# One table of places for the side work of a fused FNet and GEGLU kernel, up to the second block of gate and up

## The chip, the cores and the metric

The kernel runs on one core of one Trainium2 chip. The metric is the device time of one execution in microseconds (us); where several executions were timed, their median is given.

## What is computed

The reference takes 2048 tokens of 448 features through two residual layers:

```
x  = A_x
n  = layernorm(x)
a  = n @ dft_hid_re.T          b = n @ dft_hid_im.T
h  = x + dft_seq_re @ a - dft_seq_im @ b
m  = layernorm(h)
h2 = h + (gelu_tanh(m @ w_gate) * (m @ w_up)) @ w_down      # 448 -> 1792 -> 448
```

## The kernel before

**Arithmetic.** Every operand is kept as two f16 parts, high and low, and a product takes three matmuls (high by high, high by low, low by high). Most products are made in the seven-product way of Strassen, so that operands are first added and subtracted among each other. The high part is a copy on ScalarE (ACT), L108 (`hi_part`), the low part a subtraction on VectorE (DVE), L112 or L114 (`lo_part`), the sums run on VectorE (L263 to L272 for tokens, L357 to L380 for the weights of gate and up, L510 to L512 for the sequence matrix, L616 to L619 for the tokens of the fast units) or on GpSimd (POOL; L232 to L235 for down's weights). SyncE (SP) issues all DMAs in one queue.

**First stage: 64 units** (`N_STEPS`), counted by `n`. A unit is a chunk of the sequence DFT: its matrix chunk `wr` is loaded (`seq_load`, L471), split into `ws` and multiplied with the normalized tokens `xs`. Units 0 to 31 are 24 plain matmuls of 448 columns (`seq_mm`, L682). Units 32 to 63 (`FAST` on) are 42 matmuls of 224 columns (`fast_mm`, L560); for each of them VectorE makes `sums` (L510 to L512) and the low parts of `ws` (L114), ScalarE the high parts. Results go out as `zs`, are turned by four DMA transposes (`z_turn`, L707) and multiplied with the hidden DFT in groups of 21 matmuls (`hid_mm`, L768, into a bank `y` that `hid_seed`, L749, fills first and `hid_out`, L757 to L759, empties), which gives the rows `h` of eight token tiles, q and j.

**Second stage: gate and up.** `GateUp(t)` for t = 0 to 41: block 0 (t = 0 to 13) has 1024 tokens in matmuls of 512 columns, the blocks 1 and 2 (t = 14 to 27, 28 to 41) have 512 each in matmuls of 256. One t is `x1, z1, y1, x2, z2, y2, y3` (L1112), where `y3` of t comes behind `x1` and `z1` of t + 1. ScalarE and VectorE empty the banks between: `pY` from `pX` (L1157), `m5` (L1163), `u2` (L1168), `g1` (L1173), `c12` and `hs` (`plus`, L1122; L1191), GpSimd multiplies (L1206). The hidden activations `hs` are written to DRAM (L1212). In blocks 1 and 2 the down projection (`dn_mm`, L1316) is woven in.

**Side work.** What prepares later operands has to be put between these products: in block 0 the split of gate and up's weights (`Weights`: raw load, `tails`, `sums`, `hi`, `rest`, `lo`, `store`) for the even chunks 2 to 12, the split of down's weights `wd` (`down_load`, `down_sums`, `down_hi`, `down_lo`), and the operands of the second block's tokens (`ffn_bias`, `ffn_norm_act`, `ffn_sums`, `ffn_hi`, `ffn_lo`, and four DMA transposes `ffn_transpose`, L327, into `hops`). The token tile of q = 2, j = 0 is named `xn_2_0`, `tt_2_0`, `xs_2_0`.

**What sets the order.** No scheduler moves anything: an engine runs its instructions in the order in which the program text records them. In the first stage tables (`W_AT` for weights, `P_AT` for turns and hidden products, `F_AT` for tokens' operands, `T_AT` for the fast units' second tiles) say at which place a step is recorded: places 3n, 3n + 1 and 3n + 2 lie before unit n, after its first half and after its end. In the second stage three ways stand beside each other: the weights' steps and down's steps are written out in the loop over t (`w`, `n`, `PREP_AT`), and the tokens' steps go by `AT_A` and `AT_B` with `do(t, k)`.

Of the kernel before, what the change touches and what calls it, by code (L numbers as in the profile page):

```python
# [32 lines left out]
def kernel(  # L33
# [1307 lines left out]
    side = {}  # L1341

    def do(t, k):
        for what in side.pop((t, k), ()):
            what()
# [4 lines left out]
    AT_B = ((0, 1), (0, 3), (1, 1), (1, 3), (2, 1), (2, 2), (2, 3), (2, 3))  # L1350
    AT_B += ((3, 2), (3, 3), (4, 1), (4, 3), (4, 4), (5, 1), (5, 4), (6, 4))
    for q, t0, step, when in ((2, 5, 3, AT_A), (3, 14, 6, AT_B)):
        for j in range(2):
            plan = (
                lambda q=q, j=j: ffn_bias(q, j),
                lambda q=q, j=j: ffn_norm_act(q, j, hp[q, j]),
                lambda q=q, j=j: ffn_sums(q, j, (0,)),
                lambda q=q, j=j: ffn_hi(q, j, (0,)),
                lambda q=q, j=j: ffn_sums(q, j, (1,)),
                lambda q=q, j=j: ffn_lo(q, j, (0,)),  # L1360
                lambda q=q, j=j: ffn_hi(q, j, (1,)),
                lambda q=q, j=j: ffn_sums(q, j, (2,)),
                lambda q=q, j=j: ffn_transpose(q, j, (0,)),
                lambda q=q, j=j: (ffn_lo(q, j, (1,)), ffn_sums(q, j, (3,))),
                lambda q=q, j=j: ffn_lo(q, j, (2,)),
                lambda q=q, j=j: ffn_transpose(q, j, (1,)),
                lambda q=q, j=j: ffn_hi(q, j, (2,)),
                lambda q=q, j=j: ffn_transpose(q, j, (3,)),
                lambda q=q, j=j: ffn_lo(q, j, (3,)),
                lambda q=q, j=j: ffn_transpose(q, j, (2,)),  # L1370
            )
            for (f, k), what in zip(when, plan):
                at(side, (t0 + step * j + f, k), what)

# [281 lines left out]
```

## Time and profile before

| what | value |
|---|---|
| median of 3 executions | 702.33 us (701.72 to 702.81) |
| the profiled execution | 703.34 us |
| its span on the core | 701.6 us |
| granted TensorE clock | 0.999 |
| PE busy | 689.0 us, 98% |
| DVE busy | 579.9 us, 83% |
| ACT busy | 417.2 us, 59% |
| POOL busy | 109.8 us, 16% |
| DMA moved | 155.43 MB |

Busy time is the time in which an engine has an instruction under way. A matmul of the profile lasts until its modelled end, so two neighbours overlap. In the views below, a wait is the idle time of an engine just before an instruction, with the engine and line that ended it; a timeline row has the start, the duration, the engine, the line, operation, what is written and read, how many instructions were merged, and in brackets the idle time before.

### The profile page before, as it was taken

To read this page: it belongs to the slowest core of one execution; us is meant where nothing else is said; L and a number is where in the kernel's file an instruction comes from. 1 tells how busy PE (TensorE), PEld (TensorE's weight loads), DVE (VectorE), ACT (ScalarE), POOL (GpSimd) and SP (SyncE) were. 2 spreads that over 40 slices of the span, in tenths; PEclk is the share of its full clock that TensorE was granted. 3 is DMA by queue.
4 is the path that set the end of the run, shared out by engine and by line. 5 is a ranking of instruction groups with operands and counts; after the bars stand their busy time and mean duration, and the time that the engine had idled before them with its cause. 6 is when DMAs were issued, how large, how long until landed. Compare 5 with 4: busy or idle time off the path is not lost. (4 is left out here: it accounts for less than half of the span.)

```text
span 701.6 us, 13978 instructions
## 1 busy us (share of the span) xinstructions
PE 689.0 (98%) x5266; PEld 508.7 (73%) x5266; DVE 579.9 (83%) x1203; ACT 417.2 (59%) x855; POOL 109.8 (16%) x127
## 2 busy tenths in 40 slices
PE   9999999999999999999999999999999999999998
PEld 5555555554979879887744444459999999999997
DVE  7998799948999798997548999976788876899786
ACT  5776677837766475664637778556555454555631
POOL 0000001010100100000213333421020111232224
PEclk9999999999999999999999999999999999999999
DMA  8788559797887729675564679797899985887612
GB/s 283 248 227 282 155 207 269 247 258 264 182 204 164 187 92 175 203 180 185 150 227 138 244 258 322 193 308 247 238 255 257 320 275 178 309 303 265 243 40 81
DMA packets 115781, 155.43 MB, mean 222 GB/s; under 512 B 63744, under 2 KB 80256, under 8 KB 115712
## 3 DMA queue, kind: packets, MB, share of 16 engines
q1 hardware_dynamic: 115712, 154.53, 72.9%
q8 instruction: 41, 0.67, 0.4%
q14 instruction: 28, 0.23, 0.1%
HBM read 105.74 MB, written 34.34 MB: 200 GB/s over the span
## 5 line engine op out<-in xcount | busy, mean ns | idle before, releaser
L1112 PEld LDWEIGHTS <-gw 128*128 128x128 f16 x1330 | 129.9, 98 | 44.5 <-issue 3.4
L682 PE MATMUL acc<-xs,ws 128*128 128x448 f16 x768 | 146.5, 352 | 0.4 <-DVE xs L149 0.4
L560 PEld LDWEIGHTS <-ws 128*128 128x128 f16 x1344 | 128.1, 98 | 7.5 <-DVE ws L114 5.8
L682 PEld LDWEIGHTS <-ws 128*128 128x128 f16 x768 | 75.1, 98 | 70.5 <-issue 0.3
L1316 PE MATMUL acc_d<-wd,dn_w 128*128 128x224 f16 x1008 | 110.8, 259 | 0.3 <-DVE dn_w L112 0.3
L1316 PEld LDWEIGHTS <-dn_w 128*128 128x128 f16 x1008 | 96.8, 98 | 2.7 <-DVE dn_w L112 0.5
L1206 POOL TENSOR_TENSOR hs<-hs,c 128x256 f32<-128x256 f32 (+1 forms) x42 | 60.1, 1431 | 244.7 <-ACT c L1204 212.5
L560 PE MATMUL acc_f<-t,ws 128*128 128x224 f16 x768 | 93.0, 259 | 1.7 <-DVE ws L114 1.7
L1112 PE MATMUL pY<-hops,gw 128*128 128x256 f16 (+1 forms) x560 | 85.6, 294 | 2.3 <-ACT u L1168 1.5
L114 DVE SCALAR_TENSOR_TENSOR ws<-wr,ws 128x768 f16<-128x768 f32 (+2 forms) x66 | 69.8, 1059 | 8.4 <-ACT ws L108 8.4
L560 PE MATMUL acc_f<-xs,ws 128*128 128x224 f16 x576 | 74.0, 259 | 1.7 <-DVE ws L114 1.7
L108 ACT ACTIVATE ws<-wr 128x768 f16<-128x768 f32 (+2 forms) x66 | 60.4, 916 | 15.0 <-DMA wr<-in_w_seq_dram 14.1
L768 PE MATMUL y<-wh,z 128*128 128x448 f16 x336 | 66.2, 352 | 1.1 <-ACT y L749 1.1
L1112 PE MATMUL pX<-hops,gw 128*128 128x256 f16 (+1 forms) x385 | 61.7, 294 | 0.0
L1112 PE MATMUL pZ<-hops,gw 128*128 128x256 f16 (+1 forms) x385 | 61.7, 294 | 0.0
L768 PEld LDWEIGHTS <-z 128*128 128x128 f16 x336 | 32.9, 98 | 30.6 <-issue 1.3
L108 ACT ACTIVATE ws<-sums 128x512 f16<-128x512 f32 x64 | 39.0, 624 | 24.4 <-DVE sums L510 19.3
L1157 ACT ACTIVATE pY<-pX 128x256 f32<-128x256 f32 (+1 forms) x42 | 18.4, 439 | 56.4 <-PE pX L1112 56.4
L1122 DVE SCALAR_TENSOR_TENSOR c<-pZ,u 128x256 f32<-128x256 f32 (+1 forms) x42 | 21.4, 510 | 36.0 <-PE pZ L1112 18.3
L1112 PEld LDWEIGHTS <-gu_w 128*128 128x128 f16 x266 | 26.0, 98 | 31.8 <-issue 0.9
L213 POOL TENSOR_SCALAR r_h<-mv_h 128x2 f32<-128x2 f32 x7 | 1.7, 240 | 267.0 <-ACT y L759 266.9
L1168 ACT ACTIVATE u<-pY 128x256 f32<-128x256 f32 (+1 forms) x42 | 19.1, 454 | 40.7 <-PE pY L1112 40.3
(160 smaller groups left out, 1023.3 us busy)
## 6 DMA issues: line engine op xcount, KB each, us to landing
gw<-w_dram SPq DMA_DIRECT2D x35, 896.0 KB, 6.7
wr<-in_w_seq_dram SPq DMA_DIRECT2D x100, 256.0 KB, 4.1
hid_dram<-hs SPq DMA_DIRECT2D x27, 512.0 KB, 6.3
hid<-hid_dram SPq DMA_DIRECT2D x54, 256.0 KB, 5.4
w_dram<-gu_w SPq DMA_DIRECT2D x14, 896.0 KB, 4.7
wr<-in_w_seq_dram SPq DMA_DIRECT2D x14, 512.0 KB, 5.5
gu_raw<-in_w_gu_dram SPq DMA_DIRECT2D x14, 384.0 KB, 5.5
gu_raw<-in_w_gu_dram SPq DMA_DIRECT2D x14, 320.0 KB, 5.1
```

Of the source, the lines that this page charges most:

```text
L108: A.activation(dst, src, AF.Copy, scale=scale)
L114: V.scalar_tensor_tensor(dst, src, scale, hi, op0=ALU.mult, op1=ALU.subtract)
L213: G.tensor_scalar(r[:, 1], mv[:, :, 1], D * EPS, -0.5 / (D * X_SC**2), op0=ALU.add, op1=ALU.mult)
L560: PE.matmul(fast_sum(n, k), fast_a(n, i, lw, a), fast_b(j, lx, b), start=j == 0 and m == 0 and k in (0, 1, 3, 5), stop=j == NT // 2 - 1 an ...
L682: PE.matmul(acc[key][:, :D], w[:, lw, block * P : (block + 1) * P], xs[c][:, lx, :], start=c == 0 and m == 0, stop=c == NT - 1 and m == 2,)
L768: PE.matmul(y[:, :D], z[p][:, lz, k, g * P : (g + 1) * P], wh[:, lw, k, :], start=p == NP - 1 and k == 0 and m == 0, stop=k == 6 and m == ...
L1112: PE.matmul(ps, w[:, wo, :], ops[:, OPS[b] + m, :], start=first and n == 0, stop=last and n == len(W_TERMS[a]) - 1, skip_group_check=True,)
L1122: V.scalar_tensor_tensor(dst, ps, SC, other, op0=ALU.mult, op1=ALU.add)
L1157: A.activation(self.Y, self.X, AF.Copy)
L1168: A.activation(self.u2, self.Y, AF.Copy, scale=SC)
L1206: G.tensor_mul(c22, c22, self.cols(self.c12))
L1316: PE.matmul(ps, w[:, la, a, :], wd[n][:, lb, b, :], start=n == 0 and m == 0 and opens, stop=n == NC - 1 and m == 2, skip_group_check=True,)
```

## The change

All side work up to the second block of gate and up now stands in the tables, and one list `slots` carries it through both stages. The second stage has eight places for each t: place 192 + 8t + k, with k = 0 before `y1`, 1 behind `y1`, 2 behind `x2`, 3 behind `z2`, 4 behind `y2`, 5 behind `x1` of t + 1, 6 and 7 at the end of t. The steps of the even weight chunks are rows of `W_AT` now, down's weights have a table `D_AT`, the second and third block's tokens a table `H_AT`, and `do(q)` is called at each place. Nothing is computed that was not computed before, and no step is left out: the instructions are the same on every engine. What differs is where some of them stand: `rest` of a weight chunk now comes ahead of the low parts of the raw weights; in the first stage second tiles (`T_AT`), turns and hidden products (`P_AT`), tokens' operands (`F_AT`) and chunks 0 and 1 (`W_AT`) have other numbers; in the second stage the tokens of q = 2 and down's first and last chunks stand elsewhere.

```diff
     W_AT = {
...
-        1: (0, 70, 79, 81, 84, 84, 87, 87, 91),
-        0: (0, 79, 88, 90, 96, 96, 99, 99, 106),
+        1: (0, 70, 79, 81, 84, 84, 84, 87, 87, 88),
+        0: (0, 78, 87, 89, 95, 95, 95, 99, 99, 106),
+        2: (2, 175, 192, 192, 193, 193, 194, 194, 197, 198),
...
     P_AT = {
...
-        4: (121, 120, 126, 133, 145, 150, 148),
-        5: (145, 144, 150, 157, 169, 186, 172),
+        4: (120, 119, 125, 132, 144, 149, 153),
+        5: (147, 147, 152, 159, 170, 187, 173),
...
     F_AT = {
...
-        2: (108, 111, 114, 114, 114, 114, 114, 114, 114, 114, 118, 119, 121, 122),
+        2: (108, 111, 111, 111, 111, 111, 111, 111, 111, 111, 116, 119, 121, 124),
...
     T_AT = {
...
-        2: (63, 86, 88),
+        2: (68, 92, 94),
...
+    H_AT = {
+        4: (225, 226, 228, 230, 230, 231, 233, 233, 248, 245, 251, 256, 252, 256, 252, 260),
+        5: (259, 260, 268, 273, 273, 274, 276, 276, 281, 284, 284, 289, 285, 289, 285, 293),
...
+    D_AT = {
+        0: (192, 195, 203, 204, 203, 206, 206),
...
+    FFN = 3 * N_STEPS
+    JIT_F = [f for f, when in W_AT.items() if f == 0 or when[4] >= FFN]
...
             lambda f=f: gu[f].hi(True),
-            lambda f=f: (gu[f].lo(True), gu[f].rest()),
+            lambda f=f: gu[f].rest(),
+            lambda f=f: gu[f].lo(True),
             lambda f=f: gu[f].hi(False),
...
+    for n, when in D_AT.items():
+        plan = (
+            lambda n=n: down_load(n),
+            lambda n=n: down_sums(n),
+            lambda n=n: down_hi(n, 0),
+            lambda n=n: down_lo(n, 0),
+            lambda n=n: down_hi(n, 1),
+            lambda n=n: down_lo(n, 1, slice(0, 2)),
+            lambda n=n: down_lo(n, 1, slice(2, 5)),
+        )
...
+    for p, when in H_AT.items():
+        o = divmod(p, 2)
+        plan = (
+            lambda o=o: ffn_bias(*o),
+            lambda o=o: ffn_norm_act(*o, hp[o]),
+            lambda o=o: ffn_sums(*o, (0,)),
+            lambda o=o: ffn_hi(*o, (0,)),
...
+    def do(q):
+        for what in slots.pop(q, ()):
+            what()
...
-    AT_A = ((0, 1), (0, 2), (0, 3), (1, 1), (1, 1), (1, 2), (1, 3), (1, 3))
-    AT_A += ((2, 1), (2, 3), (2, 3), (3, 1), (2, 4), (3, 1), (2, 4), (3, 4))
...
-        if w:
-            w.tails()
-            w.sums()
+        do(FFN + 8 * t)
         cur.y1()
...
+        do(FFN + 8 * t + 1)
         cur.x2()
-        if n is not None:
-            down_hi(n, 1)
...
+        do(FFN + 8 * t + 2)
         cur.z2()
-        do(t, 1)
+        do(FFN + 8 * t + 3)
         cur.y2()
-        do(t, 2)
+        do(FFN + 8 * t + 4)
         cur.c_last()
```

Three places show how instructions moved. The first is ScalarE in the first stage, ahead of the sums of unit 33, where the bank of the hidden product `y_2_1` gets its seed (`t2_3` are second tiles of the fast units, `gu_w1` the split weights of chunk 1). Before:

```order
L108 ACTIVATE gu_w1_1803<-gu_raw1_1526 128x256
L108 ACTIVATE t2_3_1834<-tx2_1353 128x448 x2
L108 ACTIVATE gu_w1_1803<-gu_s1_1744 128x768
L108 ACTIVATE gu_w1_1803<-gu_s1_1744 128x640
L757 ACTIVATE hx1_0_1646,mv_h1_0_1876<-y_2_0_1738 128x448
L758 ACTIVATE mv_h1_0_1876<-mv_h1_0_1876 128x1
L759 ACTIVATE y_2_0_1738,mv_h1_0_1876<-y_2_0_1738,mv_h1_0_1876 128x448
L749 ACTIVATE y_2_1_1880<-hx1_0_1646 128x448
L108 ACTIVATE gu_raw0_1717<-gu_raw0_1717 64x128 x2
L108 ACTIVATE ws33_0_1899<-wr33_1732 128x768
```

Now:

```order
L108 ACTIVATE gu_w1_1803<-gu_raw1_1519 128x256
L108 ACTIVATE gu_w1_1803<-gu_s1_1741 128x768
L108 ACTIVATE gu_w1_1803<-gu_s1_1741 128x640
L108 ACTIVATE gu_raw0_1701<-gu_raw0_1701 64x128 x2
L757 ACTIVATE hx1_0_1663,mv_h1_0_1875<-y_2_0_1761 128x448
L758 ACTIVATE mv_h1_0_1875<-mv_h1_0_1875 128x1
L759 ACTIVATE y_2_0_1761,mv_h1_0_1875<-y_2_0_1761,mv_h1_0_1875 128x448
L749 ACTIVATE y_2_1_1879<-hx1_0_1663 128x448
L108 ACTIVATE ws33_0_1900<-wr33_1730 128x768
L108 ACTIVATE ws33_1_1901<-sums33_1899 128x512 x2
L108 ACTIVATE t2_3_1937<-tx2_1471 128x448 x2
```

The two copies into `t2_3` moved from ahead of the seed to behind it, and two short copies of chunk 0's raw weights moved ahead of it.

The second is SyncE's queue in the fast units, where the matrix chunk of unit 45 (`wr45`) is loaded (`hops0<-xs_1_0` turns a token tile's operands, `z4<-zs4` the result of units 32 to 39). Before:

```order
L742 DMA hx2_0_2630<-in_x_dram 128x2x448
L707 DMA_TRANSPOSE z4_2653<-zs4_2235 128x7x128 x4
L327 DMA_TRANSPOSE hops0_1616<-xs_1_0_2454 128x4x128
L327 DMA_TRANSPOSE hops0_1616<-xs_1_0_2454 128x12x128
L471 DMA wr45_2692<-in_w_seq_dram 128x512 x2
```

Now:

```order
L471 DMA wr44_2620<-in_w_seq_dram 128x512 x2
L707 DMA_TRANSPOSE z4_2632<-zs4_2235 128x7x128 x4
L327 DMA_TRANSPOSE hops0_1665<-xs_1_0_2398 128x4x128
L471 DMA wr45_2691<-in_w_seq_dram 128x512 x2
L327 DMA_TRANSPOSE hops0_1665<-xs_1_0_2398 128x12x128
```

The load moved ahead of the widest of the four transposes.

The third is VectorE in block 0, t = 4 and 5 (`gu_w6` are split weights, `wd2` down's weights, `hs` the hidden activations, `tt_2_0` and `xs_2_0` the second block's first token tile). Before:

```order
L1122 SCALAR_TENSOR_TENSOR hs_4_4735<-pY_4_4663,m5_4_4678 128x4x128
L114 SCALAR_TENSOR_TENSOR gu_w6_4710<-gu_s6_4698,gu_w6_4710 128x384
L114 SCALAR_TENSOR_TENSOR gu_w6_4710<-gu_s6_4698,gu_w6_4710 64x3x128
L114 SCALAR_TENSOR_TENSOR gu_w6_4710<-gu_s6_4698,gu_w6_4710 64x128
L114 SCALAR_TENSOR_TENSOR gu_w6_4710<-gu_s6_4698,gu_w6_4710 128x256
L1191 SCALAR_TENSOR_TENSOR hs_4_4735<-pY_4_4663,g1_4_4720 128x4x128
L114 SCALAR_TENSOR_TENSOR wd2_4268<-wd32_2_4523,wd2_4268 128x448
L1122 SCALAR_TENSOR_TENSOR c12_5_4806<-pZ_5_4760,u2_5_4787 128x512
L243 SCALAR_TENSOR_TENSOR mv_h2_0_2924<-mv_h2_0_2924,r_h2_0_3316 128x2
L1122 SCALAR_TENSOR_TENSOR hs_5_4809<-pY_5_4745,m5_5_4766 128x4x128
```

Now, from the first of the four `gu_w6` on:

```order
L114 SCALAR_TENSOR_TENSOR gu_w6_4710<-gu_s6_4698,gu_w6_4710 128x384
L114 SCALAR_TENSOR_TENSOR gu_w6_4710<-gu_s6_4698,gu_w6_4710 64x3x128
L114 SCALAR_TENSOR_TENSOR gu_w6_4710<-gu_s6_4698,gu_w6_4710 64x128
L114 SCALAR_TENSOR_TENSOR gu_w6_4710<-gu_s6_4698,gu_w6_4710 128x256
L265 TENSOR_TENSOR tt_2_0_4746<-xn_h2_0_4728 128x192
L266 TENSOR_TENSOR tt_2_0_4746<-xn_h2_0_4728,tt_2_0_4746 128x192
L112 TENSOR_TENSOR xs_2_0_4778<-xn_h2_0_4728,xs_2_0_4778 128x2x64
L112 TENSOR_TENSOR xs_2_0_4778<-xn_h2_0_4728,xs_2_0_4778 128x2x192
L1248 SCALAR_TENSOR_TENSOR hs_4_4739<-pY_4_4663,g1_4_4721 128x4x128
L114 SCALAR_TENSOR_TENSOR wd2_4262<-wd32_2_4523,wd2_4262 128x448
L268 TENSOR_TENSOR tt_2_0_4746<-xn_h2_0_4728,tt_2_0_4746 128x192
L1179 SCALAR_TENSOR_TENSOR c12_5_4824<-pZ_5_4766,u2_5_4801 128x512
```

Five instructions of the second block's tokens came in here, and one more (L263) stands just ahead of the first `gu_w6`; `hs_5` follows `c12_5` at once, and the short one of L243 has gone further up.

More of the change, by code (lines that the diff above doesn't have):

```diff
@@ L882 @@
             put(q, what)
-    for f, n in zip(JIT_F, (6, 5)):
-        put(3 * (N_STEPS - n) + 1, lambda f=f: gu.update({f: Weights(f, f % 3)}))
-    put(3 * (N_STEPS - 3) + 2, lambda: gw_first(1))
+    if 1 not in JIT_F:
+        put(GW1, lambda: gw_first(1))
+    for n, when in D_AT.items():
[8 more added lines that the diff above has]
+        )
+        for q, what in zip(when, plan):
+            put(q, what)
+    for p, when in H_AT.items():
[5 more added lines that the diff above has]
+            lambda o=o: ffn_hi(*o, (0,)),
+            lambda o=o: ffn_sums(*o, (1,)),
+            lambda o=o: ffn_lo(*o, (0,)),
+            lambda o=o: ffn_hi(*o, (1,)),
+            lambda o=o: ffn_sums(*o, (2,)),
+            lambda o=o: ffn_transpose(*o, (0,)),
+            lambda o=o: (ffn_lo(*o, (1,)), ffn_sums(*o, (3,))),
+            lambda o=o: ffn_lo(*o, (2,)),
+            lambda o=o: ffn_transpose(*o, (1,)),
+            lambda o=o: ffn_hi(*o, (2,)),
+            lambda o=o: ffn_transpose(*o, (3,)),
+            lambda o=o: ffn_lo(*o, (3,)),
+            lambda o=o: ffn_transpose(*o, (2,)),
+        )
+        for q, what in zip(when, plan):
+            put(q, what)
+    def do(q):
+        for what in slots.pop(q, ()):
+            what()
     put(3 * (N_STEPS - 1), gelu_table)
-    put(3 * (N_STEPS - 2) + 1, lambda: (down_load(0), down_load(1)))
     fast_at = [FAST + n for n in (-4, -2, -1)] + list(range(FAST + 1, N_STEPS - 2))
@@ L967 @@
             x_lo(n + 2)
-        for what in slots.pop(3 * n, ()):
-            what()
+        do(3 * n)
         if n >= FAST:
@@ L991 @@
                 if m in (6, 13):
-                    for what in slots.pop(3 * n + 1 + m // 7, ()):
-                        what()
+                    do(3 * n + 1 + m // 7)
             continue
@@ L1021 @@
                     z_out(*key)
-            for what in slots.pop(3 * n + 1 + half, ()):
-                what()
-    assert not slots, sorted(slots)
+            do(3 * n + 1 + half)
+    assert min(slots) >= FFN, min(slots)
     last_lo.pop()()
     z_turn(NP - 1)
-    down_sums(0)
     h_tile(NB - 1, 1)
@@ L1338, in dn_store @@
         nc.sync.dma_start(outr[p // 4, p % 4], hr[p])
[L1341 to L1345, printed above, removed]
-    AT_A = ((0, 1), (0, 2), (0, 3), (1, 1), (1, 1), (1, 2), (1, 3), (1, 3))
-    AT_A += ((2, 1), (2, 3), (2, 3), (3, 1), (2, 4), (3, 1), (2, 4), (3, 4))
[L1350 to L1373, printed above, removed]
     right.close()
@@ L1398 @@
                 hid_load(d)
-        if t > 0 and w is None:
+        if t + 2 not in JIT_F:
             gw_load(t + 2)
@@ L1435 @@
         cur.x1()
-        if w:
-            w.lo(False)
-            gw[t + 2] = w.w
-        if n is not None:
-            for part in W_LO1:
-                down_lo(n, 1, part)
-        if t + 1 in PREP_AT and t > 0:
-            down_sums(PREP_AT[t + 1])
+        do(FFN + 8 * t + 5)
         if t == NF - 1:
@@ L1467 @@
             dn_sums(2)
-        do(t, 3)
-        if w:
-            w.store()
-        if w and w.f + 4 in JIT_F:
-            gu[w.f + 4] = Weights(w.f + 4, (w.f + 4) % 3)
-        if n is not None and 2 <= n + 2 < NC:
-            down_load(n + 2)
-        do(t, 4)
+        do(FFN + 8 * t + 6)
+        do(FFN + 8 * t + 7)
     COUNT = (1, 2, 1, 2, 1, 1, 2, 1, 2, 1, 2, 1, 2, 2)
@@ L1503 @@
             prev.store()
+        do(FFN + 8 * t)
         cur.y1()
@@ L1506 @@
             cur.z1()
+        do(FFN + 8 * t + 1)
         cur.x2()
@@ L1512 @@
             dn_hi(split)
+        do(FFN + 8 * t + 2)
         cur.z2()
-        do(t, 1)
+        do(FFN + 8 * t + 3)
         cur.y2()
@@ L1543 @@
             dn_sums(d)
-        do(t, 2)
-        do(t, 3)
-        do(t, 4)
+        for k in range(4, 8):
+            do(FFN + 8 * t + k)
         for p, t0 in ended.items():
```

33 lines of the change are left out of this document (11 added, 22 removed), and 37 rows, old and new, of tables (D_AT, F_AT, H_AT, P_AT).

## The prediction

> **What bounds the kernel now.** I read the page's busy times first:
>
> ```profile
> PE 689.0 (98%) x5266; PEld 508.7 (73%) x5266; DVE 579.9 (83%) x1203; ACT 417.2 (59%) x855; POOL 109.8 (16%) x127
> ```
>
> TensorE has work under way for 98% of the span and its instructions don't change, so only its waits can be won. They are few. These are PE's waits in the stretches 160 to 230, 230 to 300 and 395 to 460 us, in this order (total, times, longest):
>
> ```profile
> PE acc_f L560 <- DVE ws L114: 1.2, 2, 0.8
> PE y L768 <- ACT y L749: 1.1, 1, 1.1
> ...
> PE acc_f L560 <- DVE ws L114: 2.2, 6, 0.5
> ...
> PE pY L1112 <- ACT u L1168: 1.0, 1, 1.0
> PE pY L1112 <- ACT pY L1157: 0.4, 1, 0.4
> PE pY L1112 <- DVE hs L1122: 0.4, 1, 0.4
> ```
>
> A wait costs more than its idle time, because a matmul's modelled end overlaps the next one. In the chain of waits 102 matmuls of 224 columns take 9.75 us, one each 96 ns, while the group gives each 259 ns:
>
> ```profile
> 669.77 9.75 PE acc_d L1316 x102
> ...
> L1316 PE MATMUL acc_d<-wd,dn_w 128*128 128x224 f16 x1008 | 110.8, 259 | 0.3 <-DVE dn_w L112 0.3
> ```
>
> So 259 - 96 = 0.163 us of every wait is hidden in the busy time. With it the three stretches hold 2.3 + 3 x 0.163 = 2.8 us, 2.2 + 6 x 0.163 = 3.2 us and 1.8 + 3 x 0.163 = 2.3 us: 8.3 us in all. That is the most that this change can win.
>
> **Stretch A, 160 to 230 us (term -1.5).** ScalarE and VectorE here, from two timelines, and VectorE's load in 180 to 200 us (third number pair):
>
> ```profile
> 165.50 1.04 ACT L108 ACTIVATE t<-tx 128x448 f16<-128x448 f32 x2 [2.08 <-DMA w_dram<-gu_w]
> 166.44 1.45 ACT L108 ACTIVATE gu_w<-gu_s 128x768 f16<-128x768 f32 x2
> 169.44 0.55 ACT L749 ACTIVATE y<-hx 128x448 f32<-128x448 f32 x1
> 170.02 0.64 ACT L108 ACTIVATE gu_raw<-gu_raw 64x128 f32<-64x128 f32 x2
> ...
> 167.93 1.79 DVE L114 SCALAR_TENSOR_TENSOR gu_w<-gu_s,gu_w 128x384 f16<-128x384 f32 x4 [2.03 <-ACT gu_w L108]
> ...
> 180.00:200.00 20.00, 18.79 (x174) 16.37 (x173) 19.38 (x38) 12.60 (x28) 2.46 (x6) 1.00 1.07 210
> ```
>
> ScalarE stands 2.08 us for the store that frees `t2_3`'s buffer, then copies for 166.44 - 165.50 = 0.94 us; behind it wait chunk 1's copies and the seed at 169.44, for which TensorE waits 1.1. With the copies behind the seed 3.0 us go, and chunk 0's two copies of 0.64 come in ahead of it: the seed comes 2.4 earlier, so its wait of 1.1 + 0.16 goes. VectorE had sat 2.03 us for the same copies and was then 97% busy (19.38 of 20) up to the wait for `ws` at 192; it starts that run 2.03 earlier. TensorE arrives 1.3 earlier, so of the 1.2 + 0.33 there 1.5 + 1.3 - 2.03 = 0.8 stays. That makes 2.8 - 0.8 = 2.0. The loads of `wr31` and `wr32`, on which this stretch starts, and two transposes of `hops0` also changed places in SyncE's queue, which may shift it either way. I take -1.5, bounds -0.5 to -2.8, the whole of what the stretch holds.
>
> **Stretch B, 230 to 300 us (term -1.9).** SyncE's queue and VectorE's waits:
>
> ```profile
> 229.84 2.83 SPq L327 DMA_TRANSPOSE hops<-xs  x2
> ...
> 238.14 0.69 DVE L510 TENSOR_TENSOR sums<-wr 128x512 f32<-128x512 f32 x1 [4.69 <-DMA wr<-in_w_seq_dram]
> ...
> 266.42 7.28 SPq L707 DMA_TRANSPOSE z<-zs  x4
> 275.10 1.00 SPq L471 DMA_DIRECT2D wr<-in_w_seq_dram  x2
> ...
> 279.12 0.69 DVE L510 TENSOR_TENSOR sums<-wr 128x512 f32<-128x512 f32 x1 [2.06 <-DMA wr<-in_w_seq_dram]
> 285.82 0.69 DVE L510 TENSOR_TENSOR sums<-wr 128x512 f32<-128x512 f32 x1 [1.07 <-DMA wr<-in_w_seq_dram]
> ```
>
> VectorE sits 4.69 us for `wr45` and only then falls behind TensorE. The load now stands ahead of the wider of two transposes that took 2.83 us of SyncE; by their widths (12 and 4) it goes up by 2.83 x 12/16 = 2.1 us, so VectorE's sitting shrinks to about 2.6 and its chain starts 2.1 earlier. The moves in `F_AT` and `P_AT` put VectorE's work for tokens ahead of other sums; they fill no other idle time and I cost them at nothing. Later `wr53` goes ahead of four `z` transposes of 7.28 us, so the wait of 2.06 goes; `wr54` stays behind them, and its 1.07 grows as VectorE comes earlier. Of the 3.2 us 1.1 stays if all the 2.1 is kept; part of what is won at 242 to 257 comes back at 264 to 290, where TensorE now arrives earlier than the late `wr54`. I take -1.9, bounds -0.5 to -3.2.
>
> **Stretch C, block 0 (term -1.0).** First VectorE before the waits near 426 and ScalarE before the one of 1.0 at 449; then VectorE at t = 4 and 5, the same four `gu_w` instructions at t = 8, TensorE behind `hs`, and durations for what moves (minimum, median and maximum; then means of forms):
>
> ```profile
> 419.38 0.75 DVE L112 TENSOR_TENSOR xs<-tt,xs 128x576 f16<-128x576 f32 x1
> 421.08 0.68 DVE L1191 SCALAR_TENSOR_TENSOR hs<-pY,g 128x512 f32<-128x512 f32 x1
> ...
> 448.48 0.42 ACT L108 ACTIVATE xs<-tt 128x256 f16<-128x256 f32 x1 [4.28 <-DVE tt L272]
> 448.95 0.58 ACT L1168 ACTIVATE u<-pY 128x512 f32<-128x512 f32 x1
> ...
> 393.00 4.52 DVE L114 SCALAR_TENSOR_TENSOR gu_w<-gu_s,gu_w 128x384 f16<-128x384 f32 x4
> 399.38 0.69 DVE L1122 SCALAR_TENSOR_TENSOR hs<-pY,m 128x512 f32<-128x512 f32 x1
> ...
> 426.32 1.80 DVE L114 SCALAR_TENSOR_TENSOR gu_w<-gu_s,gu_w 128x384 f16<-128x384 f32 x4
> ...
> 401.33 1.46 PE L1112 MATMUL pY<-hops,gw 128*128 128x512 f16 x6
> ...
> L263 DVE TENSOR_TENSOR tt<-xn_h x8: 347/351/1425, 124.8 to 522.8; 128x192 f32<-128x192 f32 x8
> L265 DVE TENSOR_TENSOR tt<-xn_h x8: 348/350/353, 125.1 to 529.7; 128x192 f32<-128x192 f32 x8
> ...
> L112 DVE TENSOR_TENSOR xs<-xn_h,xs 128x128 f16<-128x128 f32 x16 | 4.5, 282 | 0.0
> L112 DVE TENSOR_TENSOR xs<-xn_h,xs 128x384 f16<-128x384 f32 x8 | 4.4, 552 | 0.1
> ```
>
> Gone: from 419.38 to 421.08 VectorE works 1.7 us on `xs_2_0`, and the waits of 0.4 + 0.4 + 0.33 = 1.1 us follow; that work now lies an iteration earlier. ScalarE stands 4.28 us for `xs_2_1`'s last copy and `u`, for which TensorE waits 1.0 + 0.16, stands behind it; the copy has moved behind the next t's `pY`. That makes -2.3. What is late next: `hs_5`. It ended at 399.38 + 0.69 = 400.07, and TensorE needs its bank from 401.33, a slack of 1.26. Six instructions came in ahead: L263, L265 and, of the same form, L266 and L268 of 0.35 each, and two of 0.28 and 0.55 (the first at most the 128x128 form's), together 2.23, less the short one that left. Without GpSimd in the way `hs_5` is 2.2 - 1.26 = 0.9 late at most. But the four `gu_w` take 4.52 us here and 1.80 at t = 8: the difference is GpSimd's four operations that run in between, and L263 shows one instruction of 0.35 stretched to 1.4. One such stretch makes it 2.0. I take +1.3, bounds 0.4 to 2.0, and -2.3 + 1.3 = -1.0.
>
> The Trainium skill ("SBUF — State Buffer", section on the two separate sides) says that an instruction of VectorE with two SBUF inputs and one of GpSimd lock each other out for the whole instruction. The trace agrees (1.80 against 4.52 us). By that rule every added instruction could take its turn behind one of GpSimd; that is the third rival.
>
> **The second block's start (term +0.8).** SyncE before it; its four transposes between 440 and 470 us with their first and last start, and their time to landing (minimum, median, maximum); the first product that reads them; VectorE's last instruction on `hs_11`; SyncE's waits for such; and the median landing of such stores there:
>
> ```profile
> 450.61 6.47 SPq L327 DMA_TRANSPOSE hops<-xs  x3
> ...
> L327 SPq DMA_TRANSPOSE hops<-xs x4: 1260/2439/3417, 438.8 to 455.8; - x4
> ...
> DMA to landing us min/median/max: 2.5/5.5/5.9
> ...
> 467.05 0.71 PE L1112 MATMUL pX<-hops,gw 128*128 128x256 f16 x5
> ...
> 454.30 0.69 DVE L1191 SCALAR_TENSOR_TENSOR hs<-pY,g 128x512 f32<-128x512 f32 x1
> ...
> SPq L1212 <- DVE hs L1191: 7.5, 3, 5.4
> ...
> hid_dram<-hs SPq DMA_DIRECT2D x3, 512.0 KB, 8.4
> ```
>
> The last three transposes of `xs_2_1` are issued from 450.61 to 457.08, the last from 455.8 (5.2 behind the first), and their product starts at 467.05. In the new table they stand behind three `hid` loads, a weight load and the store of `hs_11`, which came behind them until now, and that store waits for VectorE, here until 454.30 + 0.69 = 454.99. With stretch C's 1.0 that is 454.0, and the product is at 466.0. So the transposes are issued from 454.0 or a little later, the last 5.2 on, at 459.2 or later, and with 2.5 to 5.9 us it lands at 461.7 to 465.1: no wait. With the store's 8.4 it lands at 467.6, 1.6 late, and a late start of SyncE comes on top. So 0 to 2.2; I take 0.8, between nothing and the landing at 8.4, because the queue is fuller now where they stand.
>
> **The sum.** -1.5 - 1.9 - 1.0 + 0.8 = -3.6. The profiled execution took 703.34 us (its span 701.6 and 1.7 around it), 1.0 above the median of the three runs. The sum is a difference, so I take it off the median: 702.33 - 3.6 = 698.7 us (699.7 against the profiled one). All terms at their good ends give -2.8 - 3.2 - 1.9 + 0 = -7.9, which would need every wait of three stretches to vanish; at their bad ends -0.5 - 0.5 - 0.3 + 2.2 = +0.9.
>
> **Rivals.**
>
> *The waits only move (701.4 us, chance 0.10).* VectorE has 18 to 19 of 20 us of work in these stretches, so what it delivers earlier at 242 it may owe at 264 and 290, where `wr54` still comes late, and in block 0 `hs_5` takes what `hs_8` gave back. Then B and C are worth about nothing, the second block's start costs 0.6 and A gives 1.5: -0.9. For it speaks the busy share; against it that VectorE has 2.03 + 2.1 + 2.06 us of idle time that is really filled.
>
> *The second block starts late (704.9 us, 0.08).* One mechanism, in SyncE's queue near 455: the store of `hs_11` now stands ahead of the transposes, and SyncE's wait for such a product lasted up to 5.4 us. If the store waits so much longer than to 454.0, the transposes land at 465.1 + 5.4 = 470.5, or with the store's 8.4 at 467.6 + 5.4 = 473.0, 7.0 behind the product's 466.0: -4.4 + 7.0 = +2.6. It decides from a stall of 4.4 us on. Against it: `hs_11` is done 12 us ahead of the product in this trace, and nothing in the change delays it.
>
> The Trainium skill ("DMA: Bandwidth & Descriptors", section on queues, rings and completion order) says that each DMA engine takes descriptors in the order of its ring. [...]
>
> *VectorE and GpSimd alternate at t = 4 and 5 (701.9 us, 0.04).* If each of the four instructions behind the last `gu_w` and L263 ahead of it meets a GpSimd operation, three more are stretched by 1.07: 1.3 + 3.2 = 4.5 at `hs_5`, and the sum is -0.4. Against it: GpSimd has four operations there, and the four `gu_w` use them up already.
>
> **How the numbers follow.** The forecast has 0.78: -1.4 to -5.5, likeliest -3.6. A measurement can tell about 0.2%, 1.4 us, from no change. Faster by more than that is the forecast: 0.78. Within it lie the first and the third rival: 0.14. Slower: 0.08. The range goes from 697.0 (5.3 less) to 701.5, where it takes in the first rival and leaves out the third and the second, and about 0.07 of the forecast's own good end.
>
> **What would show it.** Right: no wait for `y` L749 near 168; the wait for `ws` near 192 below 0.8; `sums` waiting for `wr45` less than 3 us and at most one short wait between 240 and 260; none near 426 and 449; a new wait of about a microsecond on `hs` L1122's line between 396 and 402. Wrong: waits for `ws` between 260 and 292 of 2 us or more, a wait on `hops` at the first products of 256 columns above 2 us, or `wr45` landing as late as before.

## The result, and the profile after

Over 11 executions of each kernel the median went from 702.33 to 698.48 us, a ratio of 0.9948 (95% interval 0.9933 to 0.9964). The forecast was 698.7, in a range of 697.0 to 701.5. The number came out, but two of its four terms were too small a gain and one too small a cost, by a cause that it did not name; that the sum met the median is in part luck, as the account below shows.

The profiled execution of the changed kernel took 697.04 us, its span is 695.2. These are the first row of its page's busy times and all its waits of TensorE (total, times, longest, in us):

```profile
PE 687.0 (99%) x5266; PEld 509.4 (73%) x5266; DVE 575.9 (83%) x1203; ACT 416.9 (60%) x855; POOL 113.8 (16%) x127
```
```profile
PE acc_d L1373 <- DVE dn_w L112: 1.7, 1, 1.7
PE pY L1169 <- DVE hs L1179: 1.5, 2, 1.0
PE pw L102 <- POOL sign_t L93: 1.4, 1, 1.4
PE pY L1169 <- ACT u L1225: 0.4, 1, 0.4
PE acc_d L1373 <- ACT v L1107: 0.2, 1, 0.2
```

From 160 to 300 us nothing is left: no `ws`, no `y`. With the prediction's 0.163 us of hidden overlap for each wait, stretch A went from 2.8 to 0, stretch B from 3.2 to 0. In block 0 the three waits of 2.3 in all gave way to one of 1.0 + 0.16 = 1.2 on `hs`, so -1.1. The wait for `dn_w` at the second block's start went from 0.3 to 1.7, so +1.4. That is -5.7; the end has 0.3 less (0.5 to 0.2 for `v`) and the start no wait for `xs` (0.4), which makes about -6.4, as the spans have it: 695.2 - 701.6.

VectorE shows where stretches A and B were won. Its load from 160 to 180 and from 220 to 240 us (busy time is the third number), first in the kernel before, then in the changed one:

```profile
160.00:180.00 20.00, 17.64 (x33) 1.00 0.62 229
220.00:240.00 20.00, 15.04 (x24) 1.00 0.97 228
```
```profile
160.00:180.00 20.00, 19.55 (x37) 1.00 1.08 270
220.00:240.00 20.00, 18.97 (x29) 1.00 0.76 178
```

VectorE is not faster; it stands still less, 1.9 us less in the first and 3.9 less in the second. The load of `wr45` in SyncE's queue, before and now, and VectorE's sitting for it now:

```profile
232.77 3.95 SPq L471 DMA_DIRECT2D wr<-in_w_seq_dram  x6
```
```profile
226.70 1.00 SPq L471 DMA_DIRECT2D wr<-in_w_seq_dram  x2
```
```profile
230.77 0.69 DVE L510 TENSOR_TENSOR sums<-wr 128x512 f32<-128x512 f32 x1 [0.72 <-DMA wr<-in_w_seq_dram]
```

The sitting is 0.72 us where it was 4.69.

Why is the span 6.4 us shorter and the median only 3.9? The profiled execution before lies 1.0 above its median, that of the changed kernel is the fastest of its eleven. Five of the eleven have a granted clock of 0.998 and took 699.3 to 700.4 us, six have 1.0 and took 697.0 to 698.5. What the five are likely to have in common came out of the first experiment.

### The profile page after: what moved, and what is told of

The parts are those of the page before. It is cut to its first block, busy times and chain, and to the rows that moved or that the text cites. A ratio compares the mean times of both kernels' runs of the same rounds, so it can differ in the third digit from the quotient of the medians.

```text
span 695.2 us, 13978 instructions
## 1 busy us (share of the span) xinstructions
PE 687.0 (99%) x5266; PEld 509.4 (73%) x5266; DVE 575.9 (83%) x1203; ACT 416.9 (60%) x855; POOL 113.8 (16%) x127
## 4 chain that ended last, share of the span: by engine, by line
PE 91%; DVE 3%; DMA 3%; ACT 1%; issue 1%; SPq 0%; DVEq 0%; ACTq 0%
PE acc L682 21%; PE acc_f L560 19%; PE acc_d L1373 15%; PE pY L1169 12%; PE y L768 9%; PE pZ L1169 8%; PE pX L1169 8%; DVE gu_w L114 1%; DMA hid_dram<-hs 1%; DMA gw<-w_dram 1%; ACT gu_w L108 0%; DMA x<-in_x_dram 0%; SPq L327 0%; ACT u L1225 0%; DVE hs L1179 0%
## 5 line engine op out<-in xcount | busy, mean ns | idle before, releaser
L112 DVE TENSOR_TENSOR dn_w<-dn_s,dn_w 128x640 f16<-128x640 f32 x48 | 42.0, 874 | 1.6 <-ACT dn_w L108 1.6
```

Source lines behind the costliest of these rows:

```text
L112: V.tensor_sub(dst, src, hi)
```

## The experiments

Each was timed against the kernel before on the same chip; ratios are to that kernel. Numbers of places and rows are those of the changed kernel's tables.

| run | ratio | 95% interval |
|---|---|---|
| the changed kernel again | 0.9951 | 0.9936 to 0.9966 |
| changed, `t2_3` ahead of the seed | 1.0037 | 1.0022 to 1.0052 |
| changed, `F_AT` row 2 back | 0.9988 | 0.9975 to 1.0002 |
| changed, `H_AT` rows 4 and 5 back | 0.9914 | 0.9901 to 0.9928 |
| changed, `H_AT` row 5 back | 0.9918 | 0.9904 to 0.9931 |
| changed, one store on ScalarE's queue | 0.9915 | 0.9902 to 0.9929 |
| changed, rows 4 and 5 back, two copies later | 0.9921 | 0.9908 to 0.9935 |
| before, two rows of tables | 0.9945 | 0.9933 to 0.9958 |
| before, two rows and the weights' rows | 0.9924 | 0.9910 to 0.9939 |
| before, `F_AT` row 2 alone | 0.9962 | 0.9949 to 0.9975 |
| changed, store moved, six places later | 0.9904 | 0.9888 to 0.9920 |
| the last, and transposes early again | 0.9886 | 0.9869 to 0.9902 |

**The changed kernel again.**

> The changed kernel once more, unaltered, to see what of its trace is the kernel's and what is one execution's. In the two traces the waits of TensorE shrank by 6.3 us (13.2 to 6.9, start to start), but the medians by 3.85 only. Theory 1 (the waits that went are the kernel's; the profiled pair lies 1.0 above and 1.4 below its medians): the ratio to the kernel before is again 0.993 to 0.996, the waits near 168, 192, 243 to 257, 426 and 448 stay away in this trace too, those near 395 (1.18) and 467 (1.87) are there within 0.5. Rival (the stretch from 160 to 300 us was free of waits by luck of one execution, and the waits of 2 to 3 us that the forecast left there come in most executions): this trace has waits for ws of 1 us or more in sum between 190 and 292.

No wait for `ws` came back, so the rival is out: stretches A and B are free in this execution too. The wait at `dn_w` is longer than expected (2.4 + 0.16, against 1.87 "within 0.5"), and something follows it. TensorE's waits from 465 to 475 us, and that stretch in TensorE's load (busy time, count, granted clock, DMA share, GB/s):

```profile
PE acc_d L1373 <- DVE dn_w L112: 2.4, 1, 2.4
```
```profile
465.00:475.00 10.00, 7.57 (x57) 0.83 0.96 338
```

The granted clock of these 10 us is 0.83, which costs some 1.7 us beside the 2.4 + 0.16 of the wait. In the changed kernel's first trace the wait was 1.7 and the same stretch has 1.00:

```profile
465.00:475.00 10.00, 8.29 (x81) 1.00 1.03 399
```

1.7 of 698.7 us is 0.24%, which fits the clock of 0.998 that five of the six executions here have over their whole span. So executions are likely to part into two groups by what happens at that one wait; only one of the 0.998 was traced. The wait's price is 1.9 us without, and about 4.3 with the slower clock. (The kernel before has there 0.3 + 0.16.)

**`t2_3` ahead of the seed again.**

```diff
-        2: (68, 92, 94),      # T_AT
+        2: (68, 86, 88),
```

> The changed kernel with the two copies of chunk 2 to t2_3 back ahead of the seed of y_2_1 (places 86 and 88 in place of 92 and 94), nothing else undone. Theory 1 (stretch A's 2.8 us came from this move alone): the wait for y L749 near 168 and the waits for ws near 192 come back, 2.0 to 2.8 us slower than the changed kernel (or up to 6 if the copies now wait longer for the store of the chunk than they did in the kernel before). Rival (VectorE, loaded to 97% up to 192, hands on what it saves, so that the seed's delay is met by a later wait that was there anyhow): under 0.8 us slower, no wait at 168 above 0.5.

Measured 1.0037, 0.86% over the changed kernel's 0.9951, which is 6.0 us. ScalarE's copies, TensorE's bank group behind the seed, and its clock:

```profile
168.28 1.04 ACT L108 ACTIVATE t<-tx 128x448 f16<-128x448 f32 x2 [5.58 <-DMA w_dram<-gu_w]
```
```profile
173.75 6.50 PE L768 MATMUL y<-wh,z 128*128 128x448 f16 x21 [4.67 <-ACT y L749]
```
```profile
170.00:180.00 10.00, 6.25 (x21) 0.66 0.52 174
```

The copies stand 5.58 us for the store, not 2.08. SyncE shows why: the store stands behind two transposes of `hops0` that the changed kernel has moved ahead of it.

```profile
156.29 7.14 SPq L327 DMA_TRANSPOSE hops<-xs  x2
163.54 0.52 SPq L400 DMA_DIRECT2D w_dram<-gu_w  x1
```

So in the changed kernel's queue this place costs 4.7 + 0.16 for the seed, and 2.4 more for the clock behind it: the same 21 matmuls take 4.14 us in the changed kernel and 6.50 here. That is 7.3 us where 6.0 were measured; in this trace the wait at `dn_w` is 2.1 with the full clock behind it, which gives back part of what it costs in most executions of the changed kernel.

```profile
168.53 4.14 PE L768 MATMUL y<-wh,z 128*128 128x448 f16 x21
```

No wait for `ws` came behind it, against the expectation. The copies' place ahead of the seed is the cause of the wait at 168; the wait at 192 needs another.

**`F_AT` row 2 as before.**

```diff
-        2: (108, 111, 111, 111, 111, 111, 111, 111, 111, 111, 116, 119, 121, 124),
+        2: (108, 111, 114, 114, 114, 114, 114, 114, 114, 114, 118, 119, 121, 122),
```

> The changed kernel with only F_AT's row 2 as before, so that the load of wr45 stands again behind the transposes of hops0 of 4 and 12 blocks. Theory 1 (stretch B's 3.3 us came from the place of this load): VectorE waits 4 us or more for wr45 again, the waits for ws between 240 and 258 come back with 2.0 to 2.7 us in sum, and the time is 1.9 to 2.7 us longer than that of the changed kernel. Rival (VectorE's earlier work, moved in F_AT's other rows and P_AT, made the room): under 0.8 us longer, VectorE waits 4 us for wr45 and TensorE doesn't wait.

VectorE sits 3.96 us for `wr45` again, and five waits for `ws` are back (total, times, longest, from 236 to 292 us):

```profile
PE acc_f L560 <- DVE ws L114: 1.7, 5, 0.4
```

1.7 + 5 x 0.163 = 2.5 us, and the time is 0.9988 - 0.9951 = 0.37%, 2.6 us, longer. The theory holds in size, not in place: one of the five waits (0.4) stands between 240 and 258, where 2.0 to 2.7 were expected, and four (1.3) between 261 and 288. The row holds more than the load's neighbour: eight steps of ScalarE's and VectorE's on `xs_1_0` and two transposes change places with it.

**Both tiles of the second block's tokens back.**

```diff
-        4: (225, 226, 228, 230, 230, 231, 233, 233, 248, 245, 251, 256, 252, 256, 252, 260),
-        5: (259, 260, 268, 273, 273, 274, 276, 276, 281, 284, 284, 289, 285, 289, 285, 293),
+        4: (235, 236, 238, 243, 243, 244, 246, 246, 251, 254, 254, 259, 255, 259, 255, 263),
+        5: (259, 260, 262, 267, 267, 268, 270, 270, 275, 278, 278, 283, 279, 283, 279, 287),
```

> The changed kernel with the tokens' operands of the second block at their places of before (H_AT rows 4 and 5), so that of the change in blocks 0 and 1 nearly nothing is left. Theory 1 (there what is won is given back: 0.52 + 0.55 near 426 and 1.20 near 448 against 1.18 near 395 and 1.43 more near 467, together -0.3): those first three waits come back, the other two go or shrink to 0.5, and the time is within 0.7 us of the changed kernel. Rival, as in the forecast's terms (-1.0 and +0.8): 0.2 us slower than the changed kernel, with a wait at 467 as large as in it, since TensorE's earlier arrival makes it and not the order of the transposes.

Both missed. It is 0.37% faster than the changed kernel, 2.6 us, where "within 0.7" was expected. The waits that were to come back did, and from 380 on none is left at `dn_w`:

```profile
PE pY L1169 <- ACT u L1225: 1.1, 1, 1.1
PE pY L1169 <- DVE hs L1179: 0.8, 1, 0.8
PE pY L1169 <- ACT pY L1214: 0.4, 1, 0.4
```

These cost 2.3 + 0.49 = 2.8 us, against 1.2 for `hs` and 1.9 to 4.3 for `dn_w` in the changed kernel. What was missed is the price of the wait at `dn_w`, clock and all, in most executions. So this part of the change loses against the old places.

**Which part of it, and how.** In the changed kernel VectorE waits for a store, its `dn_w` stands behind that instruction, and TensorE waits for `dn_w`:

```profile
468.20 0.42 DVE L1179 SCALAR_TENSOR_TENSOR hs<-pY,m 128x256 f32<-128x256 f32 x1 [2.39 <-DMA hid_dram<-hs]
468.54 0.41 DVE L112 TENSOR_TENSOR dn_w<-hid,dn_w 128x256 f16<-128x256 f32 x1
469.01 0.56 PE L1373 MATMUL acc_d<-wd,dn_w 128*128 128x224 f16 x4 [1.71 <-DVE dn_w L112]
```

The kernel before had 0.76 us of such a wait there:

```profile
467.69 0.69 DVE L1122 SCALAR_TENSOR_TENSOR hs<-pY,m 128x512 f32<-128x512 f32 x1 [0.76 <-DMA hid_dram<-hs]
```

SyncE's queue ahead of it, and VectorE's last instruction on `hs_12`, the tile that the store writes out:

```profile
446.67 1.98 SPq L1286 DMA_DIRECT2D hid<-hid_dram  x3
448.74 0.38 SPq L1277 DMA_DIRECT2D gw<-w_dram  x1
449.23 0.53 SPq L1269 DMA_DIRECT2D hid_dram<-hs  x1
449.81 8.93 SPq L327 DMA_TRANSPOSE hops<-xs  x3
458.84 0.53 SPq L1277 DMA_DIRECT2D gw<-w_dram  x1
459.43 0.42 SPq L1384 DMA_DIRECT2D hr<-h_dram  x1
459.95 0.53 SPq L1269 DMA_DIRECT2D hid_dram<-hs  x1
```
```profile
455.51 0.68 DVE L1248 SCALAR_TENSOR_TENSOR hs<-pY,g 128x512 f32<-128x512 f32 x1
```

The data are there at 456.2; the store goes out at 459.95, behind three transposes that take 8.93 us to issue (6.47 in the kernel before, where no loads stood right ahead of them). `hs` has two buffers (`bufs=2`), so `hs_14` can't be written until the store of `hs_12` has landed, near 468.2, where VectorE's wait ends. Two experiments: the transposes back ahead of the loads, or the store on another queue.

```diff
-        5: (259, 260, 268, 273, 273, 274, 276, 276, 281, 284, 284, 289, 285, 289, 285, 293),
+        5: (259, 260, 262, 267, 267, 268, 270, 270, 275, 278, 278, 283, 279, 283, 279, 287),
```

> The changed kernel with only the later of the two tiles of the second block (H_AT row 5, xs_2_1) at its places of before, so that its last three transposes stand ahead of the three hid loads, the gw load and the store of hs_11 again. Theory 2 (in the changed kernel these transposes keep SyncE until 458.8, the store of hs_12 goes out 3.7 us after its data are there, the buffer of hs comes free late, VectorE and behind it dn_w wait, and where TensorE stands over some 2.4 us its clock is halved after it): the wait near 467 shrinks from 1.9 to 2.7 to under 0.5, no halved clock there, the wait of 1.2 near 443 comes back, that of 1.18 near 395 stays; ratio to the kernel before 0.990 to 0.992. Rival (the earlier xs_2_0 of H_AT row 4 does it as well, since its six instructions push all of VectorE back): a wait of 1.5 or more at 467, ratio 0.994 or more.

```diff
-                nc.sync.dma_start(
+                (nc.scalar if self.t == 12 else nc.sync).dma_start(
                     hid_dram[0, n][:, :, 2 * k : 2 * k + 2], hs[self.t].rearrange("p (n g) t -> p n g t", g=2)
```

> The changed kernel with one DMA moved: the store of hs_12 is issued from ScalarE's queue, ahead of u_13, and not from SyncE's behind the transposes. Theory 2: it goes out near 456.5 in place of 459.9, lands near 464.5, VectorE doesn't wait for it, the wait near 467 shrinks to under 0.8 without a halved clock; ratio 0.991 to 0.993. Rival (the transposes and loads fill the DMA engines, so that a store issued earlier lands no earlier): it lands at 467 or later, the wait at 467 stays at 1.5 us or more, ratio 0.994 or more.

Both as the theory has it: 0.9918 and 0.9915. With row 5 back the wait at `dn_w` is 0.2 and TensorE waits 0.9 for `u` again. With the store on ScalarE's queue the order of everything else is the changed kernel's, the store is issued at 456.7, VectorE has no wait for it, and the wait at `dn_w` is 0.6. In both runs every execution has the full clock. That one DMA is worth 0.9951 - 0.9915 = 0.36%, 2.5 us. First SyncE's and ScalarE's rows, then TensorE's waits from 380 to 470 us:

```profile
450.06 9.43 SPq L327 DMA_TRANSPOSE hops<-xs  x3
```
```profile
456.71 0.58 ACTq L1269 DMA_DIRECT2D hid_dram<-hs  x1
```
```profile
PE pY L1169 <- DVE hs L1179: 1.0, 1, 1.0
PE pZ L1169 <- DVE dn_w L112: 0.6, 1, 0.6
```

**Rows 4 and 5 back, but `u` free.** Row 5 as before the change except for two copies:

```diff
-        5: (259, 260, 262, 267, 267, 268, 270, 270, 275, 278, 278, 283, 279, 283, 279, 287),
+        5: (259, 260, 262, 267, 267, 268, 270, 270, 275, 278, 278, 283, 281, 283, 281, 287),
```

> H_AT rows 4 and 5 as before but for two places: the last copies of xs_2_1 to f16 (its parts 2 and 3) stand at 281 in place of 279, behind u, the transposes where they were before the change. Theory 2: the wait of 1.2 for u near 443 goes and none comes at 467, since the transposes still stand ahead of the hid loads: 0.7 to 1.2 us faster than with both rows back, ratio 0.989 to 0.991. Rival (the later copies make the transposes and what is queued behind them late): a wait of 1 us or more near 467, ratio 0.992 or more.

The rival's outcome. The wait for `u` near 443 went, and at `dn_w` one of 1.1 + 0.16 came: 0.9921, no better than 0.9914. VectorE waits 1.7 us for the store of `hs_11` here. With the transposes at their old places it is that store which stands behind them, and TensorE, no longer held up at 443, now arrives early enough to meet its landing. So a wait for a store of this queue shows or is hidden by how late TensorE is anyway.

**From the other side: parts of the change in the kernel before.**

```diff
-        2: (63, 86, 88),      # T_AT
+        2: (63, 92, 94),
-        2: (108, 111, 114, 114, 114, 114, 114, 114, 114, 114, 118, 119, 121, 122),      # F_AT
+        2: (108, 111, 111, 111, 111, 111, 111, 111, 111, 111, 116, 119, 121, 124),
```

> The kernel before with two rows of its tables changed and nothing else: the copies of chunk 2 to t2_3 at 92 and 94 (T_AT row 2), and F_AT's row 2 as in the changed kernel, which puts the load of wr45 ahead of the wide transpose. Theory 2 (these two places carry stretches A and B): the waits near 168, 192 and 242 to 257 go, those at 264 to 290 shrink or stay at 0.6 in sum; 4.5 to 6 us faster, ratio 0.9915 to 0.9935, with block 0's waits near 380, 426 and 448 as before. Rival (the other moves, of first copies, sums, seeds and transposes, made the room that these two use): waits for ws of 2 us or more in sum remain between 190 and 292, ratio 0.9945 or more.

In time it is the rival's number, 0.9945; in the trace it is split. The wait at 168 and all of stretch B are gone, its late part at 264 to 290 too. What stays is stretch A's second half:

```profile
PE acc_f L560 <- DVE ws L114: 1.4, 2, 1.0
```

1.4 + 0.33 = 1.7 us near 192. So of the 6.0 us of stretches A and B two rows carry the 1.3 at 168 and the 3.2 of B; near 192, with 1.5 before, they win nothing.

```diff
-        1: (0, 70, 79, 81, 84, 84, 87, 87, 91),      # W_AT
-        0: (0, 79, 88, 90, 96, 96, 99, 99, 106),
+        1: (0, 70, 79, 81, 84, 84, 87, 87, 88),
+        0: (0, 78, 87, 89, 95, 95, 99, 99, 106),
-            lambda f=f: (gu[f].lo(True), gu[f].rest()),
+            lambda f=f: (gu[f].rest(), gu[f].lo(True)),
```

> The kernel before with the two rows of the run with two rows changed and with the weights' part of the first stage: the ends of chunk 1 and 0 in W_AT (88 for 91; 78, 87, 89, 95 for 79, 88, 90, 96), and the rest of a chunk ahead of its first low parts. Theory 2 (the 1.7 us near 192 that the two rows left are VectorE's time, lost behind ScalarE's copies of gu_w: 0.80 + 0.32 + 0.26 of idle time between 165 and 183): the wait near 192 falls under 0.7 and the ratio to 0.991 to 0.9935. Rival (it is the seeds and transposes of P_AT that clear it, SyncE's queue near 150 to 156): the wait stays above 1.2, ratio 0.994 or more.

With these on top of the two rows the waits from 160 to 300 us are

```profile
PE acc_f L560 <- DVE ws L114: 0.4, 1, 0.4
```

and the ratio 0.9924: the theory's, 1.5 us below that of the two rows, with intervals that overlap a little. The weights' rows clear some 1.1 us of the 1.7. Which of the three edits does it was not separated.

Next the one row of `F_AT` alone:

> The kernel before with F_AT's row 2 alone, so that only the place of wr45's load and what stands with it changes. Theory 2 (stretch B is this place, whatever goes on in stretch A): the waits near 168 and 192 stay with 2.5 us or more in sum, those from 240 to 292 fall from 3.3 to under 1.0; 2.3 to 3.5 us faster than the kernel before, ratio 0.995 to 0.997. Rival (without stretch A's part VectorE comes too late to use the earlier load): 1.5 us or more stays between 240 and 292, ratio 0.9975 or more.

The theory's again: 0.9962, 2.7 us faster. From 160 to 300 us it has

```profile
PE acc_f L560 <- DVE ws L114: 1.2, 2, 0.8
PE y L768 <- ACT y L749: 0.9, 1, 0.9
```

which is stretch A as it was (2.1 + 0.49 = 2.6) and of stretch B nothing. One row of one table is 3.2 us of waits. The load's place alone, without the other steps of the row, was not tested. SyncE's queue and VectorE in this run:

```profile
228.04 1.27 SPq L327 DMA_TRANSPOSE hops<-xs  x1
229.41 1.01 SPq L471 DMA_DIRECT2D wr<-in_w_seq_dram  x2
```
```profile
233.49 0.69 DVE L510 TENSOR_TENSOR sums<-wr 128x512 f32<-128x512 f32 x1 [0.44 <-DMA wr<-in_w_seq_dram]
```

**A better version.** On top of the store on ScalarE's queue, six steps of `xs_2_0` go an iteration later, where VectorE has idle time.

```diff
-        4: (225, 226, 228, 230, 230, 231, 233, 233, 248, 245, 251, 256, 252, 256, 252, 260),
+        4: (225, 226, 233, 234, 235, 237, 238, 239, 248, 245, 251, 256, 252, 256, 252, 260),
```

> The changed kernel with the store of hs_12 on ScalarE's queue and six places of H_AT row 4 later (first sums and copies of xs_2_0 at 233 to 239 in place of 228 to 233), so that four of the six instructions that came in ahead of hs_5 stand behind it. Theory 2 (the wait of 1.2 near 395 is these instructions, and VectorE has 4.5 us of idle time an iteration later, from 413 to 426): the wait near 395 falls under 0.3, at most 0.5 comes near 420; 0.5 to 1.2 us faster than with the store alone, ratio 0.990 to 0.991. Rival (the work is late wherever it stands in block 0): a wait of 0.8 or more near 403 or 420, ratio 0.9915 or more.

The wait of 1.2 on `hs` near 395 is gone and nothing came at 403 or 420, as the theory said, but from 380 to 470 us the gain is met by a wait on the transposes themselves:

```profile
PE pZ L1169 <- DMA hops<-xs: 0.9, 1, 0.9
```

0.9904 against 0.9915 is inside the intervals. So in the last run the transposes also go back ahead of the loads; it has the store and the six places, and row 5 with the copies at 281:

> The kernel of the run before the last batch's end with six places and the store on ScalarE's queue, and row 5 of H_AT as in the run in which u was free (the copies of xs_2_1 at 281, its transposes where they stood before the change). Theory 2 (in block 0's end the two costs are one queue's: transposes behind the loads make hops late, 0.9 us near 460, and the store behind them makes dn_w late; with the transposes early and the store elsewhere both go, and u doesn't wait either): no wait of more than 0.4 between 395 and 470, ratio 0.988 to 0.990. Rival (something else is late at the second block's start once TensorE comes that early, the hid loads or the store's landing of 8 us): a wait of 0.8 or more there, ratio 0.9905 or more.

0.9886 (0.9869 to 0.9902), the lowest ratio of the study, 0.65% under the changed kernel's; from that of the run before it the intervals don't part it. Yet the rival's wait is there as well, 1.3 + 0.16 at `dn_w`, behind the store of `hs_11`, which stands behind the transposes again:

```profile
PE acc_d L1373 <- DVE dn_w L112: 1.3, 1, 1.3
```

The store of `hs_11` on ScalarE's queue too was not tried.

## Why the prediction was right in its number, point by point

**Stretch A (-1.5; measured -2.8).** That the seed's wait ends with the copies' place is shown by the run with them back, and by the two rows. The step on 192 gave "0.8 stays" by taking TensorE's earlier arrival from VectorE's gain; with the two rows alone 1.7 stayed. The failed step is that VectorE starts its run "2.03 earlier": its wait for ScalarE's `gu_w` didn't go, it shrank to 0.80, as the timeline of that run shows:

```profile
166.16 1.79 DVE L114 SCALAR_TENSOR_TENSOR gu_w<-gu_s,gu_w 128x384 f16<-128x384 f32 x4 [0.80 <-ACT gu_w L108]
```

So VectorE gains 1.2, TensorE arrives 1.3 earlier, and 192 stays as it was (1.2 + 0.33 before, 1.7 here). What clears 192 is for the most part the weights' part (rows 0 and 1 of `W_AT`, and `rest` ahead of the low parts), which takes those 1.7 to 0.56 and for which the prediction has no term there. It then took 0.5 off its own 2.0 for a queue that might shift it "either way". The store of `gu_w` does go out later, at 162.49 in place of 156.96, but with the copies behind the seed no wait of TensorE comes of it; what the other moves in that queue did was not separated.

**Stretch B (-1.9; measured -3.2).** The cause was right as far as the row goes: `F_AT` row 2, which puts the load ahead of the wide transpose, shown from both sides (2.6 us lost when undone, 2.7 gained alone). The failed step is "its sitting shrinks to about 2.6", from 12/16 of the transposes' issue time. It shrank to 0.72, and to 0.44 with the row alone. There the load goes out at 229.41 in place of 232.77, 3.4 earlier and not 2.1: 1.6 of it from its place (the narrow transpose takes 1.27 where the two took 2.83), the rest because the four `z` transposes ahead began 0.4 earlier and took 5.57 in place of 6.96. And it landed 4.1 us after its issue, not 5.4. Why those two shrank is not shown. The next step came as put down: nobody waits for `wr53`, and the sitting for `wr54` grew from 1.07 to 2.30. But "1.1 stays, part comes back at 264 to 290" did not: with the row alone VectorE still sits 1.74 and 1.21 us for these two loads and TensorE doesn't wait, so VectorE was late at 264 to 290 because it had been late at 240.

**Stretch C (-1.0; measured -1.1).** Right in each piece. The waits near 426 and 449 went, and one of 1.0 + 0.16 on `hs` came near 395 where +1.3 was put down. The four `gu_w` and L265 do take longer beside GpSimd, as costed, here 4.51 and 0.81 us:

```profile
387.23 4.51 DVE L114 SCALAR_TENSOR_TENSOR gu_w<-gu_s,gu_w 128x384 f16<-128x384 f32 x4
...
391.66 0.81 DVE L265 TENSOR_TENSOR tt<-xn_h 128x192 f32<-128x192 f32 x1
```

The third rival, more such turns, did not happen.

**The second block's start (+0.8; measured +1.4 in one trace, about +3.8 in the other).** The place, the queue and the direction were right, the victim wrong. The term looked for a wait on `hops`, and none came; it looked at the store of `hs_11` that now stands ahead of the transposes, and not at the next one, of `hs_12`, that came to stand behind them. Its late landing held up VectorE at a buffer, behind VectorE's instruction stood `dn_w`, and behind that TensorE. The sign was in the trace of before: VectorE waited 0.76 us there for such a store. That the clock falls behind a longer wait was not in the term at all. The second rival named this queue and the store of `hs_11`, with 7.0 us and a slower kernel. Its stall did not come: that store went out at 449.23 and held up nothing, and the transposes themselves held up the store of the next tile.

**The sum.** A and B were 2.6 us too small as gains, the last term 0.6 to 3.0 too small as a cost, and 0.7 came at the program's start and end, which had no term. In the changed kernel's profiled execution the small price holds, -6.4 in all; with 4.3 in place of 1.9 at `dn_w` it would be -4.0. (The repeat, where the larger price holds, has a span of 698.7, -2.9: there TensorE is 0.75 us behind the first trace already at 465 us, 0.36 of it from the program's start, with no wait more.) The profiled executions lie 1.0 above and 1.4 below their medians, and the changed kernel's median is the slowest of its six executions at the full clock. So that -3.6 met -3.85 is luck: errors of both signs, and a median on the edge between two groups. The first rival (waits only move) is false for the first stage and true for the second: of block 0's 1.1 us and the second block's start nothing was left but a loss.

## What to carry to other kernels

A step that is moved in a DMA queue is paid for by what then stands behind it, and the payer can be the next writer of a buffer on a third engine: follow each store to the tile that it frees, not only each load to its reader. An engine that has fallen behind shows many short waits, and the place to mend is the one long wait ahead of them: one row of a table ended six. And the first waits in a program hide later ones, so weigh the last one at the price that it has when nothing ahead of it holds TensorE up.

## What the runs showed of the hardware

**TensorE's clock.** After waits of 4.7, 2.6 and 2.4 us (idle time) the granted clock fell for some microseconds, after 2.1 and 1.7 it did not: 0.66 over 10 us, then 0.96 and 0.87 over two neighbouring stretches of 10, 0.83, 1.00, 1.00. In stretches of 1 us it is halved; the wait of 2.4 us in the repeat ended at 470.5:

```profile
470.00:471.00 1.00, 0.51 (x5) 0.96 0.99 351
471.00:472.00 1.00, 1.00 (x7) 0.50 1.00 375
...
474.00:475.00 1.00, 1.00 (x10) 0.83 0.68 285
```

By these shares the clock is at a half for some 3.4 us there, for 3.4 after the wait of 2.6 and for 6.8 after that of 4.7, and it falls 2.7 to 3.4 us after TensorE's last matmul, when TensorE may be at work again. So at `dn_w` a wait longer by 0.3 us (2.4 against 2.1) cost some 1.7 us more; three falls in three traces don't show that a shorter wait is always safe. The Trainium skill ("TensorE: Matmul & The Clock Gate", Part 1 on the clock gate) has the clock halved after an idle window of about 3.4 us whose start is free-running. That it halves agrees: the shares of 0.50 above. The length differs: here 2.4 us of idle time were enough.

**The issue of DMA transposes.** The same three transposes kept SyncE for 6.27 to 7.34 us in the eight traces in which they stand ahead of the second block's loads (6.47 in the kernel before), and for 8.93 to 9.93 in the six in which three loads, a weight load and a store were issued right ahead (8.93 in the changed one). So their issue time goes with their place in the queue and not with their size alone; what holds SyncE meanwhile is not shown.
